# A parallel spectral and MLP block on one core: one group's turn moves from matrix transposes to transposing transfers

## The chip, the cores and the metric

The kernel runs on one core of a Trainium2 chip. The metric is device time in microseconds of one execution. The core has a matrix engine (PE, with its weight loads listed as PEld), a vector engine (DVE), an activation engine (ACT), a general engine (POOL) and a sync engine (SP); each works through its own list of instructions in order and waits on semaphores for the others. All transfers of this kernel are issued from SP's list.

## The reference, cut to what matters

The input is x, 2048 rows of 448. It is normalised row by row to xn, and the result is the sum of x, a spectral branch and an MLP branch, both of xn:

```python
def _A_ref(x, w_r, w_i):                       # spectral branch
    X = rfft2(x); X = X * (w_r + 1j * w_i)
    return irfft2(X, s=(S, D))

def _B_ref(x, w1, w2, w3, w4):                 # MLP branch
    h = _gelu(_layernorm(x) @ w1)              # 448 x 448
    # four quarters of h's columns shifted by +1, -1, +2, -2 rows
    hs = concatenate([g0, g1, g2, g3]) @ w2    # 448 x 448
    x1 = x + hs
    return x1 + _gelu(_layernorm(x1) @ w3) @ w4    # 448 x 1792, 1792 x 448

xn = _layernorm(x)
return x + _A_ref(xn, w_r, w_i) + _B_ref(xn, w1, w2, w3, w4)
```

## The kernel before, in words

Rows are laid out so that one "tile" b (16 of them) holds every sixteenth row, 128 rows on 128 partitions. A shift by one or two rows is then a step to another tile. Tiles are handled in four groups of four: `GRP = [[14, 15, 0, 1], [2, 3, 4, 5], [6, 7, 8, 9], [10, 11, 12, 13]]`; "the third group" is tiles 6 to 9, number 2 in the code. Every matrix product that needs more than half precision is made from f16 halves: a high part and the remainder, and three products (high x high, high x low, low x high) summed in PSUM.

**First stage, w1.** For a group, `norm1` normalises the four tiles in place (POOL, DVE and ACT share them). The product with w1 needs x with its columns on the partitions, so the group has to be turned. There are two ways in the code:
- `turn_pe` and `turn_copy` (lines 400 to 417): PE transposes 128 x 128 blocks in f32 into PSUM (line 404), 16 of them for a group; ACT copies the high f16 part to the tile `xT` (line 414), DVE the remainder (line 415). Groups 0, 1 and 2 use it.
- `turn` (lines 819 to 828): ACT casts a normalised tile to f16 in SBUF (line 824), DVE writes the remainder beside it (825, 826), and SP issues one transposing transfer per tile (827), which writes all seven blocks of that tile to `xT`. Group 3 uses it.

`w1_unit(g, i)` (line 466) then runs 11 matmuls for one tile (`w1_in`, line 454), GELU on ACT (475), high part on ACT (476), remainder on DVE (477), and one transposing transfer on SP (480), which writes h of that tile, turned, to `hT`.

**w2.** `w2_mm(b, ks)` (line 486) runs three matmuls (498) for each of the named column quarters k; quarter k of tile b reads h of tile `b - SHIFT[k]` with `SHIFT = [1, -1, 2, -2]`. So tile 0 needs h of 14, 15, 1 and 2; tile 4 needs 2, 3, 5 and 6. `w2_tile` finishes a tile and adds it to x on DVE (505).

**w3, w4 and the rest.** w3 is loaded raw in four row blocks (215 and 218; `load_w3([3])` brings the last 64 rows twice in two loads), its squares are summed on ACT (243), `powers` turns the sum into two powers of two (one reduction on DVE, one matmul with ones, four small DVE instructions from line 256 on), and `w3_split` scales and splits it. The same is done for w1, w2 and w4. `front(G, fp)` (742) runs w3 for a pair of feature blocks of a 256-row half group: 22 matmuls (425), GELU (749), high part (752), remainder (753); `back` runs w4 (772). The spectral branch's middle stage goes over 16 chunks: `chunk_a` (pp, 648, pf, 655/656), `chunk_b` (px, 665, te, 670 to 673, z, 675) and `chunk_z`, `chunk_c` (zb, pu, y; 682 to 698), woven with the w3 and w4 matmuls.

**What sets the order.** The code is recorded through a scheduler, which keeps a time line of its own and orders each engine's list by readiness and priority. `with behind(key)` pins the instructions in it behind named ones. PSUM has four pools of two banks: acc, mm, tr and sp. SP's list is a queue: transfers go out in its order.

Of the kernel before, what the change touches and what calls it, by code (L numbers as in the profile page):

```python
# [12 lines left out]
F32 = mybir.dt.float32  # L13
# [108 lines left out]
def body(tc, nc, x, wf, w1, w2, w3, w4, c_g, c_n, c_small, out):  # L122
# [29 lines left out]
    def bank(tag, name):  # L152
        return ps.tile([128, 512], F32, tag=tag, bufs=2, name=name)
# [90 lines left out]

    def powers(m, n, key, tag="acc", mid=None):

        t = pc.tile([128, 2], F32, name=f"pt{key}")
        i = V.tensor_reduce(out=t[:, 0:1], in_=m[:, :n], axis=AX.X, op=ALU.add)
        after["t" + key] = (i.ins,)
        if mid:  # L250
            with behind("t" + key):
                mid()
        pm = bank(tag, f"pm{key}") if isinstance(tag, str) else tag
        i = T.matmul(pm[:, 0:1], ones, t[:, 0:1], start=True, stop=True)
        after["p" + key] = (i.ins,)
        V.tensor_scalar(out=t[:, 1:2], in0=pm[:, 0:1], scalar1=2.0 ** -58, scalar2=None, op0=ALU.max)
        e = pc.tile([128, 3], I32, name=f"pe{key}")
        V.tensor_scalar(out=e[:, 0:1], in0=t.bitcast(I32)[:, 1:2], scalar1=1, scalar2=0x7F800000,
                        op0=ALU.logical_shift_right, op1=ALU.bitwise_and)
        V.tensor_scalar(out=e[:, 1:2], in0=e[:, 0:1], scalar1=-1, scalar2=185 << 23, op0=ALU.mult, op1=ALU.add)  # L260
        i = V.tensor_scalar(out=e[:, 2:3], in0=e[:, 0:1], scalar1=1, scalar2=69 << 23, op0=ALU.mult, op1=ALU.add)
        after["s" + key] = (i.ins,)
        return e.bitcast(F32)[:, 1:2], e.bitcast(F32)[:, 2:3]
# [125 lines left out]
    after = {}  # L389

    @contextlib.contextmanager
    def behind(*key):
        key = key if len(key) > 1 else key[0]
        with contextlib.ExitStack() as st:
            for i in after[key]:
                st.enter_context(tc.issue_after(i))
            yield
# [20 lines left out]
    def T1(g, ts=range(4)):  # L418
        for t in ts:
            turn_copy(g, t, turn_pe(g, t))  # L420
# [44 lines left out]

    def w1_unit(g, i, pm=None):
        if pm is None:
            pm = bank(("tr" if g == 1 else "mm", "acc")[i // 2], f"pw1_{g}{i}")
            w1_in(g, [(i, pm)], range(4))
        c = CS[GRP[g][i]]  # L470
        pm = pm[:, :D]
        pv_ = pm.rearrange("p (k n) -> p k n", k=4)
        h = hs_buf[c % (HS if g == 3 else HS + 2)]
        with behind(0, i - 2) if g == 0 and i > 1 else contextlib.nullcontext():
            A.activation(out=pm, in_=pm, func=AF.Gelu_apprx_tanh, scale=gsc[:, c:c + 1])
        u = A.activation(out=h[:, 0, :, 0:112], in_=pv_, func=AF.Copy, scale=h1)
        v = V.scalar_tensor_tensor(out=h[:, 1, :, 0:112], in0=pv_, scalar=h1, in1=h[:, 0, :, 0:112],
                                   op0=ALU.mult, op1=ALU.subtract)
        o = h_at(g, i)
        d = SY.dma_start_transpose(out=hT[g][:, :, o:o + 128], in_=h.rearrange("p i k n -> p (i k n)"))  # L480
        after[g, i] = u.ins, v.ins
        after["h", g, i] = (d.ins,)
# [2 lines left out]

    def w2_mm(b, ks):
        if b not in w2b:
            w2b[b] = bank("sp", f"pw2_{b}")
        for k in ks:
            src, o = b - SHIFT[k], 1  # L490
            if src < 0:
                src, o = src + NB, 0
            elif src >= NB:
                src, o = src - NB, 2
            g, i = WHERE[src]
            o += h_at(g, i) - 1
            for hi, wi in ((0, 0), (0, 1), (1, 0)):
                m = T.matmul(w2b[b][:, :D], hT[g][:112, 4 * hi + k, o:o + 128], w2p[:, wi, k],  # L498
                             start=k == 2 and hi + wi == 0, stop=k == 3 and hi == 1)
        after["w2", b] = (m.ins,)  # L500
# [241 lines left out]
    def front(G, fp, tag):  # L742
        tok = slice(256 * (G % 2), 256 * (G % 2) + 256)
        pm = bank(tag, f"pw3_{G}{fp}")
        for ff in range(2):
            f = 2 * fp + ff
            mlp_in(pm[:, 256 * ff:256 * ff + 256], w3p, slice(128 * f, 128 * f + 128), x2all[:, G // 2], tok)
        with prio(EVAC):
            A.activation(out=pm, in_=pm, func=AF.Gelu_apprx_tanh, scale=r3)  # L749
            h = pw.tile([128, 2, 512], F16, tag="hf", bufs=3, name=f"hf{G}{fp}")  # L750
            with behind("te", 12) if (G, fp) == (4, 1) else contextlib.nullcontext():
                i = A.activation(out=h[:, 0], in_=pm, func=AF.Copy, scale=h3)  # L752
                j = V.scalar_tensor_tensor(out=h[:, 1], in0=pm, scalar=h3, in1=h[:, 0], op0=ALU.mult, op1=ALU.subtract)  # L753
            after["f", G, fp] = i.ins, j.ins
        hs[G, fp] = h
# [52 lines left out]
            T.matmul(wps, wsrc[:, 0:128], wsrc, start=True, stop=True)  # L808

    warm_up(WARM)  # L810
    m1, m2, m3, m4 = (pc.tile([128, n], F32, name=f"m{i}") for i, n in ((1, 4), (2, 1), (3, 4), (4, 7)))
    junk4 = row().bitcast(F16)[:, :2 * D]
    V.memset(m1, 0.0)
    V.memset(m2, 0.0)
    xTs = {}
    flat = lambda t: t.rearrange("p a n -> p (a n)")

    def turn(g):

        xTs[g] = p1.tile([128, 7, 512], F16, tag="xT", bufs=2, name=f"xT{g}")  # L820
        y = stage(f"x{g}", 8 * D, 1, F16).rearrange("p (i n) -> p i n", i=4)
        for i, b in enumerate(GRP[g]):
            h, x_ = y[:, i], xb(b)
            u = A.activation(out=h[:, 0:D], in_=x_, func=AF.Copy)
            V.tensor_tensor(out=h[:, 448:512], in0=x_[:, 384:448], in1=h[:, 384:448], op=ALU.subtract)
            v = V.tensor_tensor(out=h[:, 512:896], in0=x_[:, 0:384], in1=h[:, 0:384], op=ALU.subtract)
            d = SY.dma_start_transpose(out=xTs[g][:, :, 128 * i:128 * i + 128], in_=h)
        after["t", g], after[f"a{g}"] = (d.ins,), (u.ins, v.ins)

    def w3_split(i):  # L830
        t, cl = i % 4, slice(896 * (i // 4), 896 * (i // 4) + 896)
# [34 lines left out]
    with behind("a0", 1):  # L866
        n1.append(norm1(1, [P, V, A, V]))
    with behind("w1", 3):
        squares(m2[:112], flat(w2s[:112]))
    with behind("n", 1):  # L870
        pts = [turn_pe(1, t) for t in range(2)]
        with behind("T", 1):
# [32 lines left out]
            i = P.tensor_tensor(out=w2p[:, 1, k], in0=w2s[:112, k], in1=w2p[:, 0, k], op=ALU.subtract)  # L905
    after["w2p"] = (i.ins,)
    h_alloc(1)
    for k in range(4):
        w1_unit(1, k)
    for b in range(2):  # L910
        w2_mm(b, (2, 0))
    after["T", 2] = after["w2", 1]
    T1(2)
    with behind("h", 1, 3):
        load_w3([3])
    with behind("w2p"):
        n1[0][2]()
        n1[1][2]()
        for f in n1[2]:
            f()  # L920
    for b in range(2):
        with behind("T", 2):
            w2_tile(b, (1, 3))
    with behind("a2"):
        n1 = [norm1(3, [P, P, P, P])]
# [2 lines left out]
        for k in range(4):  # L928
            w1_unit(2, k)
    for k in range(4):  # L930
        with behind(*(("a2",), ("a2",), (2, 0), (2, 1))[k]):
            squares(m3[:, k:k + 1], w3raw[:, k])
    s3, r3 = powers(m3, 4, "3", "mm")
    h3 = pc.tile([128, 1], F32, name="h3")
    V.tensor_scalar(out=h3, in0=s3, scalar1=2.0 ** -5, scalar2=None, op0=ALU.mult)
    for b in range(2, 4):
        w2_tile(b)
    turn(3)
    for f in n1[0]:
        f()  # L940
# [126 lines left out]
```

## Time and profile before

| | |
|---|---|
| median of 3 runs | 413.42 us (413.39 to 413.44) |
| the profiled execution, its own time | 413.43 us |
| its span in the trace | 411.7 us |
| PE busy | 406.6 us |
| DVE busy | 295.9 us |
| ACT busy | 247.4 us |
| POOL busy | 115.1 us |
| granted clock of PE | 1.00 throughout |

Times in the trace are microseconds from the span's start. A row of a time line gives start, duration, engine, line of the kernel, operation, what it writes and reads, and a count when equal ones follow each other; in square brackets stands the idle time of the engine before it and what ended it. A row of the chain gives start, time spent and engine with line. A row of a group ends with the busy time, the mean ns of one, and the idle time before them. A row of the transfers gives the count, the size and the median time from issue to landing. Matmuls overlap, so the duration of one in a row is longer than the distance to the next one's start; distances of starts are the better measure.

### The profile page before, as it was taken

How to read it: one execution, taken by the hardware profiler on the slowest of the kernel's cores; microseconds unless marked ns; L12 is line 12 of the kernel's file. 1: busy time of each engine (PE TensorE's matmuls, PEld its weight loads, DVE VectorE, ACT ScalarE, POOL GpSimd, SP SyncE). 2: the span in 40 equal slices, each digit the busy share in tenths (PEclk: the TensorE clock that was granted, in tenths of full speed). 3: DMA queues.
4: the chain of work that ended last, by engine and by line, in shares of the span. 5: the costliest groups of instructions: out<-in, count | busy, mean ns of one | idle time of the engine just before them, and what ended most of it. 6: DMA issues, size and time to landing. Idle time of an engine off the chain costs nothing.

```text
span 411.7 us, 8524 instructions
## 1 busy us (share of the span) xinstructions
PE 406.6 (99%) x3310; PEld 290.2 (70%) x3310; DVE 295.9 (72%) x636; ACT 247.4 (60%) x427; POOL 115.1 (28%) x205
## 2 busy tenths in 40 slices
PE   8999999999999999999999999999999999999996
PEld 3555555765677877776887887777776776677885
DVE  5999999897745658863689889875776787667122
ACT  4697979963738766862678888863343434342321
POOL 2987810112307745400031221111212221221000
PEclk9999999999999999999999999999999999999999
DMA  8979599806911283437066555620000213223001
GB/s 280 363 221 199 99 172 328 188 2 140 175 47 48 88 276 129 131 72 164 13 157 170 146 146 141 158 65 2 2 0 2 68 48 110 91 69 133 24 0 46
DMA packets 53496, 48.53 MB, mean 118 GB/s; under 512 B 37600, under 2 KB 48480, under 8 KB 53456
## 3 DMA queue, kind: packets, MB, share of 16 engines
q1 hardware_dynamic: 53456, 47.99, 43.5%
q8 instruction: 26, 0.43, 0.4%
q14 instruction: 14, 0.11, 0.1%
HBM read 35.52 MB, written 3.67 MB: 95 GB/s over the span
## 4 chain that ended last, share of the span: by engine, by line
PE 91%; ACT 4%; DVE 3%; issue 1%; POOL 0%; DVEq 0%; POOLq 0%
PE pw L425 30%; PE acc L772 29%; PE pw L498 9%; PE pw L454 8%; PE ps L591 3%; PE pe L714 2%; PE py L736 2%; PE wps L808 2%; PE pp L648 2%; ACT te L670 2%; PE pu L694 1%; PE px L665 1%; PE pta L404 1%; DVE te L673 1%; ACT zb L682 1%
## 5 line engine op out<-in xcount | busy, mean ns | idle before, releaser
L425 PE MATMUL pw<-x2mem,w3p 128*128 128x256 f16 x1232 | 149.0, 272 | 0.0
L772 PE MATMUL acc<-w4p,hf 128*128 128x448 f16 (+1 forms) x714 | 138.3, 341 | 0.0
L425 PEld LDWEIGHTS <-w3p 128*128 128x128 f16 x1232 | 118.6, 98 | 18.8
L772 PEld LDWEIGHTS <-hf 128*128 128x128 f16 x714 | 69.4, 98 | 48.2 <-DVE hf L753 0.4
L749 ACT ACTIVATE pw<-pw,pe 128x512 f32<-128x512 f32 x56 | 36.8, 656 | 65.6 <-PE pw L425 65.5
L753 DVE SCALAR_TENSOR_TENSOR hf<-pw,h,hf 128x512 f16<-128x512 f32 x56 | 41.8, 749 | 42.6 <-ACT hf L752 42.2
L498 PE MATMUL pw<-w2p,h 112*128 112x448 f16 x192 | 39.1, 352 | 0.0
L752 ACT ACTIVATE hf<-pw,h 128x512 f16<-128x512 f32 x56 | 38.3, 685 | 1.2
L675 POOL TENSOR_TENSOR z<-te 128x450 f32<-128x450 f32 x16 | 16.0, 1000 | 73.7 <-DVE te L673 73.7
L454 PE MATMUL pw<-w1p,xT 128*128 128x448 f16 x176 | 35.1, 352 | 0.3 <-ACT xT L414 0.3
L721 POOL TENSOR_TENSOR e<-e 128x226 f32<-128x226 f32 x16 | 11.3, 707 | 78.2 <-ACT e L718 75.2
L498 PEld LDWEIGHTS <-h 112*128 112x128 f16 x192 | 18.6, 98 | 16.4 <-DMA h<-x2mem 0.3
L454 PEld LDWEIGHTS <-xT 128*128 128x128 f16 x176 | 17.1, 99 | 16.0 <-ACT xT L414 0.5
L655 ACT ACTIVATE pf<-pp 64x450 f16<-64x450 f32 x32 | 17.3, 541 | 15.8 <-PE pp L648 7.8
L718 ACT ACTIVATE e<-pe 128x452 f32<-128x452 f32 x16 | 8.8, 548 | 26.5 <-PE pe L714 26.5
L656 DVE TENSOR_TENSOR pf<-pp,pf 64x450 f16<-64x450 f32 x32 | 19.9, 622 | 5.3 <-ACT pf L655 5.0
L571 POOL TENSOR_TENSOR xr<-xf 128x452 f32<-128x452 f32 x8 | 9.2, 1153 | 31.1 <-issue 27.7
L670 ACT ACTIVATE te<-px 64x450 f32<-64x450 f32 x32 | 17.2, 539 | 0.5
L729 DVE TENSOR_TENSOR vh<-e,vh 128x448 f16<-128x448 f32 x16 | 10.0, 625 | 9.7 <-ACT vh L728 9.7
L574 POOL TENSOR_TENSOR f<-xr 128x452 f32<-128x452 f32 x16 | 16.1, 1028 | 0.6
L582 DVE TENSOR_TENSOR xh<-f,xh 128x452 f16<-128x452 f32 x16 | 11.8, 782 | 5.0 <-ACT xh L581 5.0
L723 DVE TENSOR_TENSOR e<-e 128x113 f32<-128x113 f32 x16 | 9.5, 594 | 7.8 <-POOL e L721 7.8
(169 smaller groups left out, 603.3 us busy)
## 6 DMA issues: line engine op xcount, KB each, us to landing
wc<-wf SPq DMA_DIRECT2D x32, 225.0 KB, 3.7
wl<-wf SPq DMA_DIRECT2D x8, 450.0 KB, 3.8
xf<-x SPq DMA_DIRECT2D x8, 448.0 KB, 3.6
xt<-x SPq DMA_DIRECT2D x3, 896.0 KB, 11.1
w3raw<-w SPq DMA_DIRECT2D x3, 896.0 KB, 14.1
xr<-x SPq DMA_DIRECT2D x12, 224.0 KB, 2.6
out<-xr SPq DMA_DIRECT2D x12, 224.0 KB, 2.0
gn<-c_g SPq DMA_DIRECT2D x16, 128.0 KB, 3.2
```

What stands on the lines that cost most here:

```text
L425: T.matmul(ps_out, wp[:, wi + t, cols], xT[:, xi + t, tok], start=t == 0 and wi + xi == 0, stop=t == 3 and wi == 4)
L454: m = T.matmul(pm[:, :D], xTs[g][:, xi + t, 128 * i:128 * i + 128], w1p[:, wi + t], start=t == 0 and p == 0, stop=t == 3 and p == 2)
L498: m = T.matmul(w2b[b][:, :D], hT[g][:112, 4 * hi + k, o:o + 128], w2p[:, wi, k], start=k == 2 and hi + wi == 0, stop=k == 3 and hi == 1)
L574: P.tensor_tensor(out=f[:, :, k:k + 2].rearrange("p b s d -> p s b d"), in0=u[:, :, 0], in1=u[:, :, 1], op=op)
L655: A.activation(out=hi, in_=src, func=AF.Copy)
L656: V.tensor_tensor(out=lo, in0=src, in1=hi, op=ALU.subtract)
L670: i = A.activation(out=e[64 * h:64 * h + 64], in_=px_[64 - 64 * h:128 - 64 * h, :2 * DF], func=AF.Copy)
L675: P.tensor_tensor(out=z, in0=t[:, 0], in1=t[:, 1], op=ALU.add)
L749: A.activation(out=pm, in_=pm, func=AF.Gelu_apprx_tanh, scale=r3)
L752: i = A.activation(out=h[:, 0], in_=pm, func=AF.Copy, scale=h3)
L753: j = V.scalar_tensor_tensor(out=h[:, 1], in0=pm, scalar=h3, in1=h[:, 0], op0=ALU.mult, op1=ALU.subtract)
L772: m = T.matmul(to, h[:, hi, o:o + 128], w4p[0][:, wi, f, r], start=f == 0 and n == 0, stop=f == 13 and n == 2)
```

## The change: what it does

1. The third group is turned by `turn(2)` in place of `T1(2)`: four casts, eight remainders and four transposing transfers in place of 16 transposes and eight evacuations from PSUM. `turn` now takes staging buffer g - 2, so the two groups that use it have one each. In the code it stands behind unit 0 of the second group; in the built order its four transfers go out between h of units 1 and 2 of that group.
2. The first four tiles of w2 are cut in parts around w1 of the third group: quarters 2 and 0 of tiles 0, 1 and 2 and quarter 2 of tile 3 are named first, quarters 1 and 3 of tiles 0 and 1 then, all behind w1 of the second group; the rest of tiles 2 and 3 comes later. In the built order 39 matmuls of w2 stand between w1 of the second and of the third group, 24 before. Tiles 2 and 3 take mm banks, w1 of the third group tr banks. The high and low halves of units 2 and 3 of the second group are pinned behind the third group's casts (`behind("a2")`).
3. In `powers` the lower guard of the norm (a maximum with 2^-58 behind the matmul) becomes a small number, 2^-65, in one more column of the sums; the shift reads PSUM directly. Memsets at the start prepare those columns.
4. In `front`, the GELU of unit (4, 1) is pinned behind te of chunk 12 as its halves already were; the halves of unit (4, 2) are pinned behind te of chunk 14.

```diff
     def powers(m, n, key, tag="acc", mid=None):
-        t = pc.tile([128, 2], F32, name=f"pt{key}")
-        i = V.tensor_reduce(out=t[:, 0:1], in_=m[:, :n], axis=AX.X, op=ALU.add)
+        t = pc.tile([128, 1], F32, name=f"pt{key}")
+        i = V.tensor_reduce(out=t, in_=m[:, :n + 1], axis=AX.X, op=ALU.add)
...
-        i = T.matmul(pm[:, 0:1], ones, t[:, 0:1], start=True, stop=True)
+        i = T.matmul(pm[:, 0:1], ones, t, start=True, stop=True)
...
-        V.tensor_scalar(out=t[:, 1:2], in0=pm[:, 0:1], scalar1=2.0 ** -58, scalar2=None, op0=ALU.max)
...
-        V.tensor_scalar(out=e[:, 0:1], in0=t.bitcast(I32)[:, 1:2], scalar1=1, scalar2=0x7F800000,
+        V.tensor_scalar(out=e[:, 0:1], in0=pm.bitcast(I32)[:, 0:1], scalar1=1, scalar2=0x7F800000,
...
     def w1_unit(g, i, pm=None):
-            pm = bank(("tr" if g == 1 else "mm", "acc")[i // 2], f"pw1_{g}{i}")
-            w1_in(g, [(i, pm)], range(4))
+            pm = bank(("tr" if g < 3 else "mm", "acc")[i // 2], f"pw1_{g}{i}")
+            after["u", g, i] = (w1_in(g, [(i, pm)], range(4)).ins,)
...
-        u = A.activation(out=h[:, 0, :, 0:112], in_=pv_, func=AF.Copy, scale=h1)
-        v = V.scalar_tensor_tensor(out=h[:, 1, :, 0:112], in0=pv_, scalar=h1, in1=h[:, 0, :, 0:112],
-                                   op0=ALU.mult, op1=ALU.subtract)
+        with behind("a2") if g == 1 and i > 1 else contextlib.nullcontext():
+            u = A.activation(out=h[:, 0, :, 0:112], in_=pv_, func=AF.Copy, scale=h1)
+            v = V.scalar_tensor_tensor(out=h[:, 1, :, 0:112], in0=pv_, scalar=h1, in1=h[:, 0, :, 0:112],
+                                       op0=ALU.mult, op1=ALU.subtract)
...
-            w2b[b] = bank("sp", f"pw2_{b}")
+            w2b[b] = bank("mm" if b in (2, 3) else "sp", f"pw2_{b}")
...
-            A.activation(out=pm, in_=pm, func=AF.Gelu_apprx_tanh, scale=r3)
+            with behind("te", 12) if (G, fp) == (4, 1) else contextlib.nullcontext():
+                A.activation(out=pm, in_=pm, func=AF.Gelu_apprx_tanh, scale=r3)
...
-            with behind("te", 12) if (G, fp) == (4, 1) else contextlib.nullcontext():
+            with behind("te", 10 + 2 * fp) if (G, fp) in ((4, 1), (4, 2)) else contextlib.nullcontext():
...
-    m1, m2, m3, m4 = (pc.tile([128, n], F32, name=f"m{i}") for i, n in ((1, 4), (2, 1), (3, 4), (4, 7)))
+    m1, m2, m3, m4 = (pc.tile([128, n + 1], F32, name=f"m{i}") for i, n in ((1, 4), (2, 1), (3, 4), (4, 7)))
...
-    V.memset(m1, 0.0)
-    V.memset(m2, 0.0)
+    for m, n in ((m1, 4), (m2, 1), (m3, 4), (m4, 7)):
+        V.memset(m, 0.0)
+        V.memset(m[:, n:], 2.0 ** -65)
...
     def turn(g):
-        y = stage(f"x{g}", 8 * D, 1, F16).rearrange("p (i n) -> p i n", i=4)
+        y = stage(f"x{g}", 8 * D, g - 2, F16).rearrange("p (i n) -> p i n", i=4)
...
     h_alloc(1)
-    for k in range(4):
+    w1_unit(1, 0)
+    turn(2)
+    for k in range(1, 4):
         w1_unit(1, k)
-    for b in range(2):
-        w2_mm(b, (2, 0))
-    after["T", 2] = after["w2", 1]
-    T1(2)
+    for b, ks in ((0, (2, 0)), (1, (2, 0)), (2, (2, 0)), (3, (2,))):
+        w2_mm(b, ks)
...
-    for b in range(2):
-        with behind("T", 2):
+    with behind("w2", 3):
+        for b in range(2):
             w2_tile(b, (1, 3))
...
     for k in range(4):
-        with behind(*(("a2",), ("a2",), (2, 0), (2, 1))[k]):
+        with behind(*((1, 3), (1, 3), (2, 0), (2, 1))[k]):
             squares(m3[:, k:k + 1], w3raw[:, k])
...
-    for b in range(2, 4):
-        w2_tile(b)
+    w2_tile(2, (1, 3))
+    w2_tile(3, (0, 1, 3))
     turn(3)
```

More of the change, by code (lines that the diff above doesn't have):

```diff
@@ L820, in turn @@
         xTs[g] = p1.tile([128, 7, 512], F16, tag="xT", bufs=2, name=f"xT{g}")
-        y = stage(f"x{g}", 8 * D, 1, F16).rearrange("p (i n) -> p i n", i=4)
+        y = stage(f"x{g}", 8 * D, g - 2, F16).rearrange("p (i n) -> p i n", i=4)
+        done = ()
         for i, b in enumerate(GRP[g]):
@@ L827, in turn @@
             d = SY.dma_start_transpose(out=xTs[g][:, :, 128 * i:128 * i + 128], in_=h)
-        after["t", g], after[f"a{g}"] = (d.ins,), (u.ins, v.ins)
+            done += (u.ins, v.ins)
+        after["t", g], after[f"a{g}"] = (d.ins,), done
     def w3_split(i):
@@ L868, in body @@
     with behind("w1", 3):
-        squares(m2[:112], flat(w2s[:112]))
+        squares(m2[:112, 0:1], flat(w2s[:112]))
     with behind("n", 1):
```

## The prediction

> **What bounds the kernel now.** I read the page's busy table and its chain first, then the chain in order of time around the change, then the queue of SP (it issues every transfer), and last the waits of PE.
>
> ```profile
> PE 406.6 (99%) x3310; PEld 290.2 (70%) x3310; DVE 295.9 (72%) x636; ACT 247.4 (60%) x427; POOL 115.1 (28%) x205
> PE 91%; ACT 4%; DVE 3%; issue 1%; POOL 0%; DVEq 0%; POOLq 0%
> ```
>
> PE is busy for 406.6 of 411.7 us and carries 91% of the chain. "Busy" alone would not prove that its matmuls stand close, so I compare starts: in the chain below twelve w2 matmuls take 2.27 us, 0.189 each, and 44 w1 matmuls 8.33, also 0.189. That pitch holds in nearly every stretch; behind the warm-up, starts fall behind it only at a handful of places, the largest of which are priced below. So the time is PE's own list of matmuls and little else: an instruction taken off PE is worth its pitch, a gap closed is worth the gap, and every new wait of PE is paid in full. There is hardly a gap to hide one in.
>
> ```profile
> 30.78 2.27 PE pw L498 x12
> 33.05 1.75 PE pta L404 x16
> ...
> 37.11 8.33 PE pw L454 x44
> ...
> 69.24 1.20 PE pw L425 x11
> ...
> 77.20 2.46 PE pw L498 x13
> ```
>
> The second row is the third group's turn on PE: 16 transposes, 1.75 us, between two pieces of w2, and w1 of that group follows at 37.11.
>
> The queue of SP in the same stretch (start, issue time, count), and what two of its windows kept busy:
>
> ```profile
> 25.85 4.11 SPq L480 DMA_TRANSPOSE h<-hs  x3
> 30.06 2.67 SPq L480 DMA_TRANSPOSE h<-x2mem  x2
> 32.82 4.06 SPq L480 DMA_TRANSPOSE h<-hs  x3
> 36.93 1.24 SPq L218 DMA_DIRECT2D w3raw<-w  x2
> 43.01 1.62 SPq L480 DMA_TRANSPOSE h<-x2mem  x1
> ...
> 69.58 1.25 SPq L480 DMA_TRANSPOSE h<-hs  x1
> ...
> 73.63 2.64 SPq L480 DMA_TRANSPOSE h<-hs  x2
> ```
>
> ```profile
> 27.00:38.00 11.00, 11.00 (x66) 6.48 (x65) 9.61 (x20) 10.38 (x19) 9.47 (x34) 1.00 1.08 191
> ...
> 61.00:70.00 9.00, 9.00 (x53) 4.96 (x52) 9.00 (x16) 8.25 (x15) 0.83 (x1) 1.00 0.96 356
> ```
>
> Five transfers from 25.85 to 32.82: one every 1.39 us, back to back, and the DMA share is 1.08 meanwhile (the column before the last): queue and DMA engines are full from 27 to 38 us. In the other window DVE (the third pair) is busy all 9.00 us. So the new transfers enter the fullest stretch of the queue, and DVE has nothing to give in the sixties.
>
> **The change, part by part.** *The 16 transposes leave PE*: -1.75 us, from the row at 33.05. PE does nothing else instead; the order of the built program shows the same matmuls otherwise. Between w1 of the second group and w1 of the third there now stand 39 w2 matmuls (24 before): 39 x 0.189 = 7.4 us of cover, from 30.78 to 38.2. The four units of w1 follow as 11 matmuls each, 2.08 us, and need their columns of xT at 38.2, 40.2, 42.3 and 44.4.
>
> *Four transfers enter SP's queue* behind the sixth h transfer. They issue at 34.2, 35.6, 37.0 and 38.4 if their sources are there. The median from issue to landing of this kind is 3.0:
>
> ```profile
> h<-hs SPq DMA_TRANSPOSE x12, 3.3
> ...
> xT<-x SPq DMA_TRANSPOSE x4, 3.0
> ```
>
> They land at 37.2, 38.6, 40.0 and 41.4: 1.0 to 3.0 us early. The sources: the transposes at 33.05 read the same normalised rows, so these are there by then at the latest, and cast and remainder of the first unit take 0.57 + 0.22 + 0.56 = 1.35 (rows below), 34.4 instead of 34.2. That leaves 0.8. I take nothing for this edge; without its cover each microsecond of lateness would be a microsecond of PE.
>
> ```profile
> L415 DVE TENSOR_TENSOR xT<-pta,xT 128x512 f16<-128x512 f32 x9 | 6.0, 684 | 0.5 <-ACT xT L414 0.5
> ...
> L824 ACT ACTIVATE x<-xt 128x448 f16<-128x448 f32 x4 | 2.3, 572 | 0.0
> L826 DVE TENSOR_TENSOR x<-xt,x 128x384 f16<-128x384 f32 x4 | 2.2, 556 | 0.0
> ...
> L825 DVE TENSOR_TENSOR x<-xt,x 128x64 f16<-128x64 f32 x4 | 0.9, 218 | 0.0
> ```
>
> On DVE four remainders from PSUM (4 x 0.68 = 2.7) become four from SBUF (4 x 0.78 = 3.1), and ACT's four copies become four casts: together under half a microsecond, in a stretch where neither bounds PE. Nothing for it.
>
> A rule speaks against this part: the Trainium skill, "VectorE: DVE Perf Modes", section "The three transpose paths", gives 390 ns for a 128x128 transpose on TensorE and 1309 ns for one by DMA, and its rules prefer TensorE where PSUM will do as the destination. The row differs: a transfer here carries seven such blocks and lands in 3.0 us, 0.43 a block, with a new one every 1.39. By the page's figure a transfer would last 7 x 1.309 = 9.2 us, an estimate, the fourth would end near 34.2 + 4 x 9.2 = 71 instead of 41.4, and PE would wait some 27 us.
>
> *What the queue does to those behind.* h of units 2 and 3 go 5.6 us later (4 x 1.39); w2's last pieces of tiles 2 and 3, which read them, now stand behind w1 of the third group, at 46.5 and later; they land near 43 and 44.4. Nothing. The two loads of w3's last rows move from 36.93 to 42.5, and the first h transfer of the third group is issued behind them, at 43.7. Before, it went at 43.01, when they had nearly landed. Does a transfer wait for the loads ahead of it? Rows of another stretch, the w3 loads' own time, and the sum of squares that reads them:
>
> ```profile
> xf<-x SPq DMA_DIRECT2D x1, 448.0 KB, 6.9
> ```
> ```profile
> x2mem<-y SPq DMA_TRANSPOSE x1, 5.5
> ```
> ```profile
> DMA to landing us min/median/max: 5.1/5.8/6.4
> ```
> ```profile
> L243 ACT ACTIVATE xr<-w3raw 128x1792 f16<-128x1792 f32 x4 | 6.8, 1692 | 0.0
> ```
>
> The first answer is of the one load issued between 101 and 102 us (at 101.2, so landed at 108.1), the second of the one transposing transfer issued between 103 and 104 (at 103.4, landed at 108.9, after 5.5 us instead of about 3): yes, it landed 0.8 us behind the load. So the second w3 load (issued 43.1, 6.4 us) lands at 49.5 and the h transfer at 50.3. PE needs it at tile 4's last third: 30.78 + 101 matmuls x 0.189 = 49.9. *A new wait of 0.4 us.* Bounds: none, if it goes past the loads (43.7 + 3.3 = 47.0); 2.9, if its 3.3 us begin only when they have landed. I take 0.4, since the two rows are the same situation. Late next to it: the squares of that w3 quarter (49.5 + 1.7 + a little = 51.4) with the norm's matmul due at 52.5, and the next h transfer, due near 54.7 and some 1 us ahead of that.
>
> *Norms guarded in the sum.* Each of the four norms loses one DVE instruction of 0.16 us between the matmul over the partitions and the scale. Six small memsets are new at the start:
>
> ```profile
> 4.28 1.16 DVE L313 BATCH_NORM_STATS2 sta<-xt 128x6 f32<-128x448 f32 x2 [2.96 <-DMA xt<-x]
> ```
> ```profile
> L256 DVE TENSOR_SCALAR pt<-pm 128x1 f32<-128x1 f32 x4 | 0.6, 156 | 1.1 <-PE pm L254 1.1
> ```
> ```profile
> PEld L454 <- DVE xT L415: 0.4, 1, 0.4
> ```
>
> The memsets lie in 2.96 us in which DVE waits for x; nothing for them. A shorter norm is worth something only where PE waits on DVE just behind it. That is one place: a weight load of w1 waited 0.4 us for the second group's remainder, which stands on DVE behind the second norm's scale. Bounds 0 and 0.4; I take 0.1, since one 0.16 goes and DVE's other work stays.
>
> *Two units' halves behind te.* In ACT's queue near 260 us, and PE's at the same time:
>
> ```profile
> 257.04 0.66 ACT L749 ACTIVATE pw<-pw,pe 128x512 f32<-128x512 f32 x1
> ...
> 258.33 1.09 ACT L670 ACTIVATE te<-px 64x450 f32<-64x450 f32 x2
> ...
> 264.63 0.64 ACT L749 ACTIVATE pw<-pw,pe 128x512 f32<-128x512 f32 x1
> 265.30 0.69 ACT L752 ACTIVATE hf<-pw,h 128x512 f16<-128x512 f32 x1
> ```
> ```profile
> 259.84 0.27 PE L648 MATMUL pp<-csm,y 113*128 113x113 f16 x2
> 260.20 0.74 PE L665 MATMUL px<-pf,gn 128*128 128x225 f16 x6
> ```
> ```profile
> 264.24 0.83 PE L694 MATMUL pu<-gn,zb 128*128 128x128 f16 x12
> 264.91 0.54 PE L772 MATMUL acc<-w4p,hf 128*128 128x448 f16 x2
> ...
> 268.51 0.83 PE L694 MATMUL pu<-gn,zb 128*128 128x128 f16 x12
> 269.57 0.74 PE L665 MATMUL px<-pf,gn 128*128 128x225 f16 x6 [0.22 <-DVE te L671]
> ...
> 270.47 1.87 PE L772 MATMUL acc<-w4p,hf 128*128 128x448 f16 x9
> ```
>
> Twelve pu matmuls take 0.67 from start to the next start (264.24 to 264.91); at 268.51 they take 1.06, so PE lost 0.39 there, waiting for te of chunk 14. At 259.84 two pp, a little narrower than a pu of 0.056, take 0.36: 0.26 lost, for te of chunk 12. The GELU of unit (4, 1) at 257.04 stands ahead of te 12 on ACT and goes behind it (0.66 earlier for te); the half of unit (4, 2) at 265.30, and its remainder on DVE, go from ahead of te 14 to behind it (another 0.6 to 0.7). Both are larger than the gaps: -0.65 in all. Queued behind the moved pieces are the pf and y evacuations, no later than before since the total is the same; PE wants hf of (4, 2) only after the matmuls of (4, 1) that start at 270.5, so 1 to 2 us after te 14 is early enough. Bounds: -0.65, and +0.3 if a half comes late.
>
> **Sum:** -1.75 - 0.1 - 0.65 + 0.4 = -2.1. The profiled execution took 413.43, its span 411.7 and 1.7 around it; the median of the runs is 413.42, the same. 413.4 - 2.1 = 411.3.
>
> **Rivals.** *The gain is kept waiting in the sixties.* After its shorter way PE asks for the fourth group's h earlier: before, the chain has tile 9's last w2 matmuls at 77.20, and they read the transfer issued at 73.63, which at 3.3 us lands at 76.9: 0.3 us to spare. In the built order of the changed kernel 205 matmuls of w1 and w2 and 37 of w3 (1.20 / 11 = 0.109 each) stand between 30.78 and the same piece, which puts it at 73.6, while DVE, full in that window, has to make the halves, the w3 remainders and the second layer norm. The order lets that transfer go right behind the one that stood at 69.58, so at about 71 (land 74.2) if DVE is no later, or a microsecond earlier if the shorter norm and the earlier tiles move DVE. So 0 to 0.6 on top of the forecast's wait as I follow the queue; if DVE or the w4 loads are a microsecond later than that, the wait eats 1 to 2 us. The time is then 412.7. For it: a full DVE and 0.3 us of slack. Against: PE found all of it in time so far, and waits do not add up, since one of 0.4 us moves all later needs by as much.
>
> *Slower: the first h of the third group and what follows.* One place, tile 4's last third at 49.9. If the transfer there starts its 3.3 us only when the loads are in, and the loads, shared with eight transfers now ending some 5 us later, take 2 us more, it lands at 54.8; the fourth group's columns and the next h queue behind it, and PE waits 5 us less what the 2.5 us of gains cover: 413.4 - 2.5 + 5 = 415.9. From a landing 2.5 us past 49.9, at 52.4, the gains are used up; 0.8 later it is measurably slower. For it: the queue's share of 1.08, and 5.5 us in the row above. Against: that row landed 0.8 behind its load.
>
> *The four transfers go one after another.* Four times 3.0 from 34.2 land the last at 46.2 instead of 44.4: 1.8 us of wait, 413.1. Against: transfers left every 1.39 us and landed in 3.3, so two or more were under way at once. By the page's rule named above it would be about 438, an estimate.
>
> **How the numbers follow.** About 0.2%, 0.8 us, is what a measurement of this kernel can tell from no change: faster is below 412.6, slower above 414.2. Forecast (411.3, its own range 410.6 to 412.3): 0.58, all faster. Kept waiting (412.7, from 412.1 to 413.5): 0.25, faster in 0.10, same in 0.15. The h transfer late: 0.13, same in 0.02, slower in 0.11. One after another: 0.01, same; a rest of 0.03 for a late half near te or a late first unit in the third group, half same and half slower. So faster 0.68, same 0.20, slower 0.12. The range begins at 410.6, all gains (1.75 + 0.4 + 0.65) and no wait, since no other work leaves PE; it ends at 413.5, with the second case inside.
>
> **What would show it.** Right: no transposes of the third group on PE, w1 of that group starting about 38.1 after 39 w2 matmuls, no gap at px near 258 and 267, a wait of PE for an h transfer of under 0.6 us near 50, and w3's first matmul on PE at about 66 (30.78 + 184 x 0.189, and the wait; 69.2 in the chain above). Wrong: PE's waits on L498 of more than 1 us, a wait on xT's transfers at 38, gaps between 70 and 90 us on h, w4 or the fourth norm, or te as late as before.

## The result and the profile after

The change makes the kernel slower by 0.4%: 415.2 us, median of 17 executions, against 413.62 for the kernel before; the ratio is 1.0039, with a 95% interval of 1.0024 to 1.0053. A second set gave 415.34 against 413.61, ratio 1.0036 (1.0024 to 1.0048). The forecast was 411.3.

The profiled execution took 415.09, its span 412.8 (411.7 before). Its busy table and its chain:

```profile
PE 404.4 (98%) x3294; PEld 287.8 (70%) x3294; DVE 295.1 (71%) x642; ACT 247.2 (60%) x427; POOL 116.2 (28%) x205
PE 81%; DMA 2%; DVE 2%; issue 0%; SPq 0%
```

PE has 16 instructions less and is busy for 2.2 us less, and still the span is longer by 1.1: PE now stands still, and transfers are in its chain, which held none before. Where, its waits between 40 and 80 us say (total us, how often, the longest; for the kernel before this view has no row):

```profile
PE pw L498 <- DMA h<-hs: 1.6, 2, 1.0
PE pw L498 <- DMA h<-x2mem: 1.4, 1, 1.4
```

PE's time line of the changed kernel shows the places (idle time before the row and its releaser in brackets; in this kernel the w1 matmuls are line 453, the transfers of `turn` line 830):

```profile
35.65 2.62 PE L498 MATMUL pw<-w2p,h 112*128 112x448 f16 x13
38.11 8.49 PE L453 MATMUL pw<-w1p,xT 128*128 128x448 f16 x44
46.44 3.57 PE L498 MATMUL pw<-w2p,h 112*128 112x448 f16 x18
51.40 0.93 PE L498 MATMUL pw<-w2p,h 112*128 112x448 f16 x4 [1.39 <-DMA h<-x2mem]
...
62.61 2.44 PE L498 MATMUL pw<-w2p,h 112*128 112x448 f16 x12 [1.05 <-DMA h<-hs]
...
75.50 0.74 PE L498 MATMUL pw<-w2p,h 112*128 112x448 f16 x3 [0.51 <-DMA h<-hs]
```

The third group's w1 starts at 38.11, as forecast. From 46.44 eighteen w2 matmuls at 0.189 end at 49.84, and the next starts at 51.40: 1.56 us lost (the bracket counts from the modelled end of the matmul ahead). By the same count 1.21 are lost before 62.61 and 0.68 before 75.50. The account of the span: -1.75 for the turn, -0.65 for te, +3.45 for the three waits make +1.05; measured are +1.1.

SP's queue in that stretch (start, issue time, count), and two rows of transfers issued between 44.5 and 46 us (the last column is from issue to landing):

```profile
34.38 5.26 SPq L830 DMA_TRANSPOSE xT<-x  x4
39.74 3.51 SPq L480 DMA_TRANSPOSE h<-hs  x2
43.31 1.22 SPq L218 DMA_DIRECT2D w3raw<-w  x2
44.63 1.26 SPq L480 DMA_TRANSPOSE h<-x2mem  x1
46.13 6.51 SPq L830 DMA_TRANSPOSE xT<-x  x3
52.73 1.26 SPq L480 DMA_TRANSPOSE h<-x2mem  x1
55.87 1.22 SPq L541 DMA_TRANSPOSE x2mem<-y  x1
57.20 1.24 SPq L830 DMA_TRANSPOSE xT<-x  x1
58.52 2.64 SPq L480 DMA_TRANSPOSE h<-hs  x2
...
62.59 2.29 SPq L229 DMA_DIRECT2D x2mem<-w  x4
69.69 6.02 SPq L480 DMA_TRANSPOSE h<-hs  x3
```
```profile
w3raw<-w SPq DMA_DIRECT2D x1, 448.0 KB, 6.6
h<-x2mem SPq DMA_TRANSPOSE x1, 6.7
```

The first h transfer of the third group goes out at 44.63 behind w3's two loads, which go out 6.4 us later than before, and takes 6.7 us instead of the 3.0 of the kernel before. Three transfers of the fourth group (x3) then take 6.51 us to issue where two took 2.6, the second h transfer follows at 52.73 instead of 50.1, and everything behind it is late. What the DMA engines do from 43 to 51 us, changed kernel first, then the kernel before (the column before the last is their busy share):

```profile
43.00:51.00 8.00, 7.01 (x38) 3.42 (x35) 7.06 (x18) 5.41 (x12) 7.21 (x19) 1.00 1.00 192
```
```profile
43.00:51.00 8.00, 8.00 (x44) 4.15 (x43) 7.76 (x21) 8.00 (x15) 7.21 (x20) 1.00 0.49 92
```

The slack that the kernel before has here, half of the DMA time, is gone.

### The profile page after: what moved, and what is told of

It reads as the page before. It is cut to its first block, busy times and chain, and to the rows that moved or that the text cites. A ratio compares the mean times of both kernels' runs of the same rounds, so it can differ in the third digit from the quotient of the medians.

```text
span 412.8 us, 8504 instructions
## 1 busy us (share of the span) xinstructions
PE 404.4 (98%) x3294; PEld 287.8 (70%) x3294; DVE 295.1 (71%) x642; ACT 247.2 (60%) x427; POOL 116.2 (28%) x205
## 4 chain that ended last, share of the span: by engine, by line
PE 81%; DMA 2%; DVE 2%; issue 0%; SPq 0%
PE pw L424 32%; PE acc L773 31%; PE pw L498 4%; PE pu L694 3%; PE ps L591 3%; PE pp L648 2%; PE pe L714 2%; PE px L665 2%; PE py L736 2%; DMA h<-hs 1%; DVE w3p L288 1%; DMA xT<-x 1%; DVE xt L505 0%; DVE stb L312 0%; DVE hs L477 0%
## 5 line engine op out<-in xcount | busy, mean ns | idle before, releaser
L582 DVE TENSOR_TENSOR xh<-f,xh 128x452 f16<-128x452 f32 x16 | 13.0, 850 | 5.0 <-ACT xh L581 5.0
```

## The experiments

Theory A: w3's two late loads hold up the transfers behind them, and the three waits are this one lateness. Theory D, formed after experiments 1, 2 and 6, which ran first: SP's order adds to it, since x3, the fourth group's transfers, stands ahead of the second h transfer. Rival B: the four new transfers, whatever the loads do.

**1. The rest of the change without the turn, and the turn without the rest.** The first kernel is the one before with these edits alone; the second has all others.

```diff
-        V.tensor_scalar(out=t[:, 1:2], in0=pm[:, 0:1], scalar1=2.0 ** -58, scalar2=None, op0=ALU.max)
...
-            with behind("te", 12) if (G, fp) == (4, 1) else contextlib.nullcontext():
+            with behind("te", 10 + 2 * fp) if (G, fp) in ((4, 1), (4, 2)) else contextlib.nullcontext():
```

The rest without the turn:

> The kernel before with the norm guard and the te order of the changed kernel, the third group still turned on PE. Theory A (the time is lost in the turn and what it moves; the rest of the change is worth what its two gone gaps, 0.26 and 0.39, say): 0.6 to 0.8 us under the kernel before, ratio 0.9982 to 0.9986, and the PE gaps at 51, 63 and 75 us that the changed kernel has are not there. Rival (these two edits are themselves part of the loss): at the kernel before or above it.

The turn without the rest:

> The kernel before with the turn by transfers and w2's parts around it, without norm guard and te order. Theory A: the changed kernel's new waits (1.56 at 51.4, 1.21 at 62.6, 0.68 at 75.5) stand there unchanged, the 1.75 of the transposes is gone, the te gaps 0.26 and 0.39 are back: +1.5 to +2.0 us against the kernel before, 0.6 above the changed one. Rival (the edits lose together only): within 0.5 us of the kernel before.

Measured: 413.02 against 413.71, ratio 0.9987 (0.9975 to 0.9999), and 415.93, ratio 1.0050 (1.0036 to 1.0063). The parts add up: -0.7 and +2.2 make +1.5. So the loss is all in the turn and what was moved with it. The waits of the second kernel are 1.62, 0.42 and 1.19 us: the first as expected, the others shared out differently.

**2. Half the load.** The second load of w3's last 64 rows is left out.

```diff
-                for h in range(2):
-                    SY.dma_start(w3raw[64 * h:64 * h + 64, 3], w3[384:448])
+                SY.dma_start(w3raw[0:64, 3], w3[384:448])
...
+    V.memset(w3raw[64:128, 3], 0.0)
```

> The changed kernel with the second of the two loads of w3's last 64 rows left out (that half of the tile is set to zero, so the output lacks the products of those rows' second half). All instructions of SP, PE and ACT keep their order. Theory A (the first wait at 51.4 us comes from the h transfer that stands behind these two loads; the waits at 62.6 and 75.5 are the same lateness handed on): the transfer lands about 2 us earlier, near 49.4, so the wait of 1.56 goes and the two behind it shrink to under 0.5 each: 2 to 3.3 us under the changed kernel, near 412. Rival B (the stretch is late because of the number of transposing transfers, whatever the loads): the first wait goes but those at 62.6 and 75.5 stay above 1 us together, and the time falls by 1.6 at most. Rival C (the lateness comes from elsewhere): no wait changes by over 0.3.

Measured: 413.28, ratio to the kernel before 0.9986 (0.9977 to 0.9995), 1.9 under the changed kernel and so between the two expectations. Its PE waits and the h transfer (window 44 to 45 us):

```profile
PE pw L498 <- DMA h<-hs: 1.0, 2, 0.6
```
```profile
h<-x2mem SPq DMA_TRANSPOSE x1, 5.4
```

The transfer takes 1.3 us less, and the wait at 51.4 is gone: it was the load. But 0.30, 0.52 and 0.81 are still lost at 60, 62 and 74 us, as rival B said, not under 0.5 each. One load less did not bring SP's queue back in time. PE's and SP's lists have the same order as in the changed kernel, here and in experiment 3.

**3. No load.** Both loads are left out.

```diff
-            else:
-                for h in range(2):
-                    SY.dma_start(w3raw[64 * h:64 * h + 64, 3], w3[384:448])
...
+    V.memset(w3raw[:, 3], 0.0)
```

> The changed kernel with both loads of w3's last 64 rows left out (these rows are set to zero, so the output lacks their products). Theory A (all three waits are the loads'): none of the three is above 0.2, the time 3.3 us under the changed kernel, 411.3 to 411.9. Theory D (SP's order makes the second and third): with the first h transfer in time and no loads in the queue there still are waits near 60 to 62 and near 74 of 0.8 to 1.6 together, 412.0 to 413.3.

Measured: 411.83, ratio 0.9953 (0.9934 to 0.9971). The largest loss left in that stretch is 0.30 us at 72.4. So with SP's order unchanged the second wait goes too, and more than half of the third: theory A for those two, while 0.3 remains for D. With three x3 transfers still ahead of it, the second h transfer went out at 49.89 and PE asked for it at 54.40, in time: x3's place costs nothing there when the queue is not backed up. This is 1.2 under the kernel without the turn (413.02): with nearly all waits away, most of the turn's 1.75 shows.

**4. The order alone.** The loads stay; x3's transfers wait for the second h transfer.

```diff
-            d = SY.dma_start_transpose(out=xTs[g][:, :, 128 * i:128 * i + 128], in_=h)
+            with behind("h", 2, 1) if g == 3 else contextlib.nullcontext():
+                d = SY.dma_start_transpose(out=xTs[g][:, :, 128 * i:128 * i + 128], in_=h)
```

> The changed kernel with the fourth group's four transposing transfers (x3) held on SP's queue until the third group's second h transfer is issued; three of them stand ahead of it otherwise. The two loads of w3 stay where they are. Theory D (the waits at 62.6 and 75.5 us come from SP's order: the three x3 transfers hold back that h transfer by some 4 us, the first y transfer waits until it has landed, and the third and fourth h transfers and w4's loads queue behind that): the h transfer issues near 47 to 50 instead of 52.7, the wait of 1.21 at 62.6 goes, the one of 0.68 at 75.5 shrinks to under 0.4, the first one of 1.56 stays: 1.2 to 1.9 us under the changed kernel, 413.3 to 414.0. Rival A (it is the loads' lateness, through ACT's square of w3's last rows at 50.6): all three waits stay within 0.3 in their sum.

Measured: 413.87, ratio 1.0001 (0.9987 to 1.0015), 1.5 under the changed kernel of the later set. The waits of PE and the queue, from an execution of 412.55, 1.3 under the median (the rows do not show what lengthens the others):

```profile
PE pw L498 <- DMA h<-x2mem: 1.4, 1, 1.4
```
```profile
44.49 6.27 SPq L480 DMA_TRANSPOSE h<-x2mem  x2
50.85 3.97 SPq L831 DMA_TRANSPOSE xT<-x  x3
54.92 2.64 SPq L480 DMA_TRANSPOSE h<-hs  x2
```

The second h transfer issues at 49.5, the third at 54.92 instead of 58.52, and the second and third wait are gone altogether. The first wait, 1.59, is untouched. ACT squares w3's last rows at 50.4, as late as in the changed kernel (50.6), so rival A's path over ACT did not make the later waits. PE's order is not the same, though: eleven w1 matmuls of the fourth group, which read x3, stand behind the twelve of w2 that read the second h, not ahead of them. So a part of the gain may be PE's new order. With that open, the two later waits need both, the loads' lateness and x3 ahead of the second h transfer, and in these runs taking away either is enough. The first needs the loads alone.

**5. The late load without the turn.** The kernel before, its loads moved behind the third group's first h transfer.

```diff
-    with behind("h", 1, 3):
-        load_w3([3])
...
+            if k == 0:
+                with behind("h", 2, 0):
+                    load_w3([3])
```

> The kernel before, third group turned on PE, with only the two loads of w3's last 64 rows moved: behind the third group's first h transfer, about 7 us later than before and later than in the changed kernel. Theory A (late loads are enough): PE waits of 1 to 3 us in the fifties and sixties, 1 to 3 us slower than before. Theory B (it takes the transposing transfers in SP's queue too): the loads land near 50 beside an emptier queue, no wait over 0.3, within 0.5 us of the kernel before.

Measured: 413.71 against 413.66, ratio 0.9999 (0.9990 to 1.0009). Its queue:

```profile
43.05 1.23 SPq L480 DMA_TRANSPOSE h<-x2mem  x1
44.33 1.22 SPq L218 DMA_DIRECT2D w3raw<-w  x2
46.85 2.56 SPq L827 DMA_TRANSPOSE xT<-x  x2
49.97 1.84 SPq L480 DMA_TRANSPOSE h<-x2mem  x1
```

The loads issue a microsecond later than in the changed kernel and cost nothing. Theory A's "late loads are enough" falls. Several things differ at once: the first h transfer is ahead of the loads, two of x3's are ahead of the second, not three, the third group's four transfers are not in the queue, PE comes 1.75 us later, and its list has the first w1 matmuls of the fourth group later than the kernel before. Which of them counts, this run alone does not show.

**6. The same move in the changed kernel.**

```diff
-    with behind("h", 1, 3):
-        load_w3([3])
...
+            if k == 0:
+                with behind("h", 2, 0):
+                    load_w3([3])
```

> The changed kernel with both loads of w3's last 64 rows moved behind the third group's first h transfer instead of ahead of it. Theory A: that transfer lands near 48, the wait at 51.4 us is gone; but ACT gets the loads' rows to square some 3 us later, and what ACT and SP do behind that is late by as much, so that the waits at 62.6 and 75.5 grow: between 1 us under and 1.5 us over the changed kernel. Rival B (number of transfers): only the first wait goes, the rest stays as it is, 1.5 us under the changed kernel.

Measured: 417.19, ratio 1.0082 (1.0068 to 1.0096), worse than either theory said. There is one wait, twice as long as the longest of the three:

```profile
55.27 3.75 PE L498 MATMUL pw<-w2p,h 112*128 112x448 f16 x12 [3.04 <-DMA h<-x2mem]
```
```profile
52.00:55.20 3.20, 0.23 (x2) 0.00 (x0) 1.86 (x5) 2.52 (x4) 0.00 (x0) 1.00 1.16 243
55.30:56.40 1.10, 1.10 (x6) 0.60 (x7) 1.03 (x4) 0.09 (x1) 0.23 (x1) 0.93 0.38 72
56.40:59.90 3.50, 3.50 (x13) 1.73 (x11) 1.45 (x6) 0.58 (x1) 0.64 (x1) 0.54 0.97 184
```

The first h transfer was in time; now PE lost 3.2 us for the second. That one stood behind the loads and three x3 transfers, but it went out at 51.98, 0.75 earlier than in the changed kernel. Its remainder was made at 49.03 (49.15 there), so theory A's path over ACT is not the reason. What moved more is when PE asks for it: at 52.07 instead of 55.90. The first wait of 1.56 is gone, and the eleven w1 matmuls of the fourth group, 2.08 us, stand behind this piece of w2, as in experiment 4. In the old order some 1.1 of the 3.2 would be left, an estimate: the first x3 transfer landed at 52.4, eleven matmuls from there end at 54.5, and the h was there at 55.2. So this run is no clean test of the queue. The third column from the end in the windows is PE's granted clock: behind the wait it fell to 0.54 for 3.5 us, and twelve matmuls took 3.75 us instead of 2.44.

**7. Another queue.** ACT issues the loads.

```diff
-                    SY.dma_start(w3raw[64 * h:64 * h + 64, 3], w3[384:448])
+                    A.dma_start(w3raw[64 * h:64 * h + 64, 3], w3[384:448])
...
-    with behind("h", 1, 3):
+    with behind("a2"):
         load_w3([3])
```

> The changed kernel with both loads of w3's last 64 rows issued by ACT, on a DMA queue of its own, once ACT has made the third group's four casts (about 34 us), instead of by SP at 43.3. Queue theory (the h transfer at 44.6 was late because it stood behind the loads on one queue): that transfer issues near 43.3 and lands near 46.5, the wait at 51.4 goes; the four xT transfers share the DMA engines with the loads and land up to 2 us later, a wait of 0 to 1.5 at 38; 412.0 to 414.5. Rival (it is the bytes, whichever queue): the third group's transfers and h transfers are each late by the 4 us that the loads take, and the sum of the waits is not smaller than the 3.45 of the changed kernel.

Measured: 419.53, ratio 1.0129 (1.0107 to 1.0151). PE waited 5.29 us before 42.5, for an h transfer that SP issued at 33.62. The transfers whose issue falls between 34 and 36 us:

```profile
w3raw<-w ACTq DMA_DIRECT2D x1, 448.0 KB, 8.2
h<-x2mem SPq DMA_TRANSPOSE x1, 8.8
h<-hs SPq DMA_TRANSPOSE x1, 7.9
```

The h transfers were not ahead of the loads on the other queue but landed with them. The rival was right that an own queue does not spare them: they share the DMA engines' time, whose share is 1.15 between 36 and 42.4 us. That the order within one queue counts for nothing does not follow. The Trainium skill, "DMA: Bandwidth & Descriptors", section "Issuing engines are not separate DMA queues", says that transfers started by different engines run on the same 16 DMA engines and interleave; the trace agrees, with 8.8 us where a transfer by itself took 3.0.

**8. Both orders mended, and a third.** w3's loads behind the first h transfer (as in 6) with x3 behind the second (as in 4); then also the y transfers of line 541 for tiles 2 and 3 behind the fourth group's third h transfer.

```diff
+            if b0 == 2:
+                late.append((b, h))
+                continue
...
+    for b, h in late:
+        with behind("h", 3, 2):
+            SY.dma_start_transpose(out=x2all[:, b // 4][:, :, 128 * (b % 4):128 * (b % 4) + 128], in_=h)
```

The first:

> The changed kernel with both orders on SP's queue mended: w3's two loads behind the third group's first h transfer, and the four x3 transfers behind its second one. From the runs before: the first h transfer lands near 46.5 instead of 51.4, the second issues near 49 and lands near 52.5 to 53. Theory (the load took the queue's time and the three x3 transfers made the second h transfer late, nothing else): no wait of PE over 0.5 between 40 and 80 us, 411.0 to 412.0, under both kernels. Rival (the loads have to land early, since ACT squares these rows ahead of the casts that the next h transfers need): a wait of 1 to 2 us moves to 53 to 60, 412.5 to 414.

The second:

> The run with both orders mended (w3's loads behind the third group's first h transfer, x3's transfers behind its second), and a third order with them: the y transfers of the second half of the first four units behind the fourth group's third h transfer instead of ahead of its first. In the run with two mended orders a wait of 1.5 us at 78.8 us came from an h transfer that stood behind such a y transfer, and one of 0.8 at 54.9 from the second h transfer. Theory: the wait of 1.5 goes and that of 0.8 stays: 411.6 to 412.6, under both kernels. Rival (the y transfers, now late, or w4's loads ahead of that h transfer take its place): a wait of 0.7 to 1.5 us behind 70 us, 412.6 to 414.

Measured: 413.88, ratio 1.0002 (0.9990 to 1.0014), and 413.37, ratio 0.9989 (0.9975 to 1.0004): neither is told apart from the kernel before, and both forecasts of a faster kernel missed. In the first, 0.80 us are lost at 54.9 and 1.53 at 78.8, where an h transfer stood behind a y transfer. In the second that wait is 0.12, but 2.08 are lost at 54.2. SP, DVE and PE there:

```profile
50.95 1.23 SPq L480 DMA_TRANSPOSE h<-x2mem  x1
52.28 1.28 SPq L836 DMA_TRANSPOSE xT<-x  x1
```
```profile
50.25 0.67 DVE L477 SCALAR_TENSOR_TENSOR x2mem<-pw,h,x2mem 128x448 f16<-128x448 f32 x1
```
```profile
46.45 5.84 PE L498 MATMUL pw<-w2p,h 112*128 112x448 f16 x30
54.20 2.44 PE L498 MATMUL pw<-w2p,h 112*128 112x448 f16 x12 [1.91 <-DMA h<-x2mem]
...
56.62 1.67 PE L453 MATMUL pw<-w1p,xT 128*128 128x448 f16 x8
```

There the second h transfer waited for nothing but its source: SP was free from 46.3 to 50.95, and DVE made the remainder (line 477) at 50.25, after the fourth group's remainders and a layer norm. The transfer took 3.2 us and so landed at 54.15; PE asked at 52.12. But in both kernels PE's order differs from the changed kernel's, as in experiments 4 and 6. Experiment 2 has that order:

```profile
46.28 5.90 PE L498 MATMUL pw<-w2p,h 112*128 112x448 f16 x30
...
52.36 2.24 PE L453 MATMUL pw<-w1p,xT 128*128 128x448 f16 x11
54.44 2.44 PE L498 MATMUL pw<-w2p,h 112*128 112x448 f16 x12
```

There the eleven w1 matmuls of the fourth group, 2.08 us, cover the time in which this h is still under way. In the second kernel they cannot stand there: they read x3, and all of x3 is held behind the second h transfer, while SP sends nothing for 4.65 us. The 2.08 us lost are just these. With the cover PE would have asked at about 54.3, after the landing (an estimate from these rows). A kernel that sends one or two x3 transfers in the free stretch, as the kernel before does at 47.00, was not run, so it is not shown that the wait cannot be avoided.

**9. One load and a copy on the chip.** x3 as in 4, one load, and POOL copies the second 64 rows (2.2 us at 51.5); the sum of squares takes only the 64 loaded rows.

```diff
-                for h in range(2):
-                    SY.dma_start(w3raw[64 * h:64 * h + 64, 3], w3[384:448])
+                SY.dma_start(w3raw[0:64, 3], w3[384:448])
...
+    with behind("c", 3):
+        P.tensor_copy(out=w3raw[64:128, 3], in_=w3raw[0:64, 3])
```

> The changed kernel with the x3 transfers behind the second h transfer and with only one of the two loads of w3's last 64 rows; POOL copies the second 64 partitions from the first (the norm's partial sums take these rows once, a power of two behind it). From the run with half the load: the first h transfer lands near 49.4, its wait goes, and with the order mended the later ones too: 411.0 to 412.0. Rival (POOL's copy, some 2 to 4 us near 51, or DVE and ACT waiting for it, makes w3's weights late): a wait of 0.5 to 3 us near 66 to 75, 412 to 414.

Measured: 413.11, ratio 0.9991 (0.9974 to 1.0009): not told apart from the kernel before, and the 411 to 412 were missed. The copy cost nothing visible; 0.90 us are lost at 53.1, again for the second h transfer (issued 49.87, landed 53.04) and again with the w1 matmuls behind it, 0.37 at 74.6, and 1.13 at 158 before a product of the spectral branch, where the changed kernel loses nothing (experiment 7 lost 1.17 before the same product, at 165.9).

**10. The changed kernel again.** 

> The changed kernel once more, beside the two mended ones: waits of 1.5, 1.2 and 0.7 at 51, 62 and 75 us again, about 1.5 us above the kernel before. Those of its executions that are over 416 show a mean granted clock of 0.997 or less, the others 0.999 to 1.000.

Measured: 415.34, waits of 1.62, 1.25 and 0.69: they repeat to 0.06. The second half of the expectation missed: the one execution over 416 (416.73) had a granted clock of 0.999.

None of these versions with the turn by transfers beats the one without it. The rest of the change alone, 413.02, has the lowest median of the kernels that leave nothing out; it is only just told apart from the kernel before (the interval ends at 0.9999), and the best with the turn, 413.11 and 413.37, are within 0.4 us of it.

## Why the prediction was wrong

*Right.* The 16 transposes were worth 1.75: w1 of the third group at 38.11 (38.1 forecast), xT's four transfers with no wait on them. They landed in this time:

```profile
xT<-x SPq DMA_TRANSPOSE x4, 3.2
```

This also settles the page's 1309 ns a block (the Trainium skill, "VectorE: DVE Perf Modes", section "The three transpose paths") for this case: seven blocks took 3.2 us, not 9.2, with the next seven 1.3 behind; its rule to prefer TensorE came out right here, for another reason than its price. The te order was worth what was said:

```profile
257.36 0.54 PE L773 MATMUL acc<-w4p,hf 128*128 128x448 f16 x2
257.73 0.74 PE L665 MATMUL px<-pf,gn 128*128 128x225 f16 x6
...
265.98 0.83 PE L694 MATMUL pu<-gn,zb 128*128 128x128 f16 x12
266.65 0.74 PE L665 MATMUL px<-pf,gn 128*128 128x225 f16 x6
```

Twelve pu take their 0.67 to the next start, two acc matmuls 0.37: no gap at px, and the first experiment's 0.7 agrees with the 0.65.

*The guard of the norms*, -0.1, brought nothing: the weight load at 24 us waits for DVE as long as before. The lower bound was the value.

```profile
PEld L453 <- DVE xT L414: 0.4, 1, 0.4
```

*The new wait at tile 4*, +0.4, was the right mechanism and mis-sized: 1.56, so this term failed by 1.2. PE asked at 49.84 (49.9 forecast) and the h transfer landed 0.8 behind the load, as its row said it would. But the load landed at 50.5, not 49.5. It was issued at 43.94 instead of 43.1, because an h transfer ahead of it took 2.16 us to issue on the full queue, not 1.3; and it took 6.6, not 6.4. I had carried queue times of the kernel before, and there the queue was not backed up at this place.

*"Waits do not add up"* is the step that failed most, by 1.9: the waits behind the first stood in the sum at nothing and measured 1.21 and 0.68. It was the argument against the rival "kept waiting", and it supposes that the transfers behind the late one go at their own time. They go in SP's order: x3's three transfers, then the second h transfer at 52.73 (50.1 before), then the first y transfer only when that has landed, 55.87, then x3's last, then the third h transfer. That made 1.21 at 62.61. w4's loads stand behind these and left 2.6 us later. The h transfer behind them went out when DVE had made its source, at 69.69 (69.58 before), but took 5.8 us instead of 3.3: 0.68 at 75.50. The rival had priced this place alone, at 0 to 0.6 by my own count and 1 to 2 if w4's loads came late, and gave 412.7; it did not combine with the first wait. The forecast's wait and the rival's came at once, and I had treated them as exclusive cases. The rival "slower" named 415.9, close to the 415.2 measured. It had the place right, and that the next h queues behind. But its time came from a transfer that starts only when the loads are in and lands at 54.8; it landed at 51.3, and the rest came from the two later waits. That the number is near is luck.

In the sum, with measured values: -1.75 + 0 - 0.65 + 1.56 + 1.21 + 0.68 = +1.05. The median rose by 1.6, 0.5 more than this. Executions of the changed kernel differ more (spans of 411.9 to 415.6, where the kernel before mostly has 411.6 to 412.2). In four of the first 17 the granted clock averaged 0.997 or less: one half-clock stretch like those in the last section lowers the mean by 0.47 x 3.4 / 412 = 0.004, an estimate. What lengthens the others stays open.

## What to carry to other kernels

Work moved from a full PE to a queue is not moved to nowhere: ask what share of the DMA engines' time is free from the move up to the next place where the queue runs empty, and price every transfer behind it up to there by the backlog, not by its time when the queue was idle. A single late transfer in an in-order queue is a whole list of late transfers, so their waits add until something lets them go out in another order. And when an engine waits for a chain through two others and a transfer, look at what other work it has meanwhile and what that work needs: in experiment 8 holding back x3 to let an h transfer go first also took from PE the 2 us of work that covered it.

## What the hardware showed

- A half-clock stretch can follow a short pause of PE. Behind the 3.2 us in experiment 6 the granted clock was 0.54 for 3.5 us, and behind the 5.29 of experiment 7 0.52. But in experiment 8's first kernel such a stretch also followed 1.48 us of pause before 9.74, 2 us later:

```profile
9.74 0.38 PE L254 MATMUL pm<-pt,ones 128*128 128x1 f32 x2 [1.31 <-DVE pt L248]
```
```profile
11.60:15.00 3.40, 3.40 (x14) 2.26 (x13) 3.40 (x7) 1.88 (x5) 2.52 (x6) 0.53 1.00 274
```

  Experiment 7's trace has the same pause (1.31 in its bracket too) and the same stretch. In experiment 9's trace the pause at this place was longer, 1.39 in its bracket or 1.55 by starts, and no such stretch followed, nor did one follow pauses of 1.56 to 2.08 us elsewhere. So the length alone does not decide. The Trainium skill, "TensorE: Matmul & The Clock Gate", section "Why this matters for your kernels", asks for no idle gaps over about 3 us; by these rows half of that is not always safe. At a clock of 0.53 such a stretch costs 3.4 x 0.47 = 1.6 us, an estimate, nearly as much as the 16 transposes.
- Two queues do not keep a transposing transfer from waiting for a load: 8.8 us from issue to landing beside two loads of 448 KB on another queue (experiment 7).
- A later stage can change with an earlier one: the 1.13 us at 158 in experiment 9 and the 1.17 in experiment 7 came with no edit there. PE waited for an addition on DVE, which stood behind a reduction that had itself waited 3.87 us for a load in the one and 3.92 in the other (2.27 in the changed kernel); why that load comes when it does was not followed.
